# Bucketed attention, a SiLU MLP and routed experts on one core: the first head's projections in two PSUM tiles, the next projection and the V loads later, and one pair's casts on GpSimd

## The chip, the core and the metric

The kernel runs on one core of a Trainium2 chip. The metric is device time in microseconds (us) of one execution, from the first instruction to the last.

## The reference, cut to what matters

Three stages follow each other. The change is in the first, and there in the work on the first of eight pairs of heads.

```python
B, H, S, D = 2, 8, 768, 64                              # attention, proj is (64, 6)
q_bits = (einsum('bhsd,dk->bhsk', q, proj) > 0)         # 6 sign bits per query
k_bits = (einsum('bhsd,dk->bhsk', k, proj) > 0)         # and per key
mask   = q_bucket[:, :, :, None] == k_bucket[:, :, None, :]   # all 6 bits equal
scores = where(mask, q @ k.T / sqrt(D), -1e9)
attn   = exp(scores - max) / (sum + 1e-9)
x      = attn @ v                                       # to (1536, 512)
x      = silu(x @ w_in) @ w_out                         # 512 -> 2048 -> 512
# then tokens with x @ w_skip > 0 go through the best of 8 experts, others pass unchanged
```

## The kernel before, in words

**Stages.** `attention` (L267 to L586) makes the attention output in SBUF, split into a rounded part and a remainder. The MLP and the experts follow, with their weights streamed in. TensorE, VectorE (DVE), ScalarE (ACT), GpSimd (POOL) and SyncE (SP, which issues most of the loads) each take their own instructions in the order of a queue.

**Pairs, units, steps.** Two heads make a pair; eight pairs (`i`), each with two halves of 384 queries, make 16 units. A unit has six steps: three tiles of 128 queries for each of two heads. The very first unit does its three tiles of head 0 first and then those of head 1 (L372); later units alternate the heads. So steps 0 to 2 are head 0 of pair 0 and steps 3 to 5 its head 1. A pair takes 12 steps.

**Scores.** To keep float32 precision, q and k are split: `kh` and `k2` are casts of k, `kl` is what the cast left off; `qa` and `qb` are casts of q, `ql` the remainder (`prep_op`, L306). A score group (`em_S`, L377) has two halves: part 0 multiplies Q1 with K1 (cast and remainder of k, 128 rows), part 1 multiplies Q2 with K2 (remainder of q with the cast of k, 64 rows, and under them 24 mark rows). The mark rows do the masking: the sign bits of query and key stand there as large numbers, such that keys of another bucket get a score far below all others. The result lies in a PSUM tile "S" of which there are two (L383), so group n + 2 needs the tile of group n, which its exponential empties.

**Marks.** For pairs from 1 on, `prep_proj` (L335) multiplies q and k of both heads by the signed projections into one PSUM tile "pj" of the ring "T" (three buffers, shared with the transposes), `marked` (L343) turns it on VectorE into marks in an SBUF tile "mb", and `prep_rows` (L346) copies the mark rows into Q2 and K2 with small DMAs on SyncE's queue. Head 0 of pair 0 has a way of its own (L490 to L504): three matmuls into a tile "pd" (K's two halves in partitions 64 and up, and 96 and up; Q's first half in partitions 0 and up), whose marks VectorE writes straight into Q2 and K2. Head 1 of pair 0, and the second half of the queries, use `prep_proj(0)` and `prep_rows(0)`: K's rows of head 1 in two DMAs, Q's rows of head 1, then Q's second half for both heads.

**Softmax.** `em_soft` (L391): the row maximum `mx` and the bias `bs` on VectorE, the exponential P on ScalarE. `em_T` (L406) transposes P in six matmuls, two steps behind the scores; a half is copied out by ScalarE, the other by VectorE. `em_PV` multiplies with V, six to eight steps behind the scores of a unit.

**Order.** The calls are written out by hand. Ahead of the loop of steps: the loads of pair 0, 29 matmuls on a zero tile (`em_busy`, whose result nobody reads), head 0's projections and casts, its marks, `prep_load(1)`, six more such matmuls, part 0 of group 0, the two ScalarE casts of head 1, `prep_proj(0)`, `prep_rows(0)`, `load_v(0)`, `load_v(1)`, head 1's GpSimd work. In step s the loop calls `em_S(s)` (part 1 alone for step 0), the first half of `em_T(s - 2)`, the casts listed in `PRE`, `em_soft(s)`, then in step 1 `k2` and `kl` of head 1 of pair 0, in steps 0 and 1 four matmuls of `em_busy`, and the second half of `em_T`. `PRE` (L519) lists for pair 1 the steps 2, 4, 6, 8 for `kh` and `qa` of either head, all on ScalarE; `POST` lists the rest. At the end of step 0 the loop calls `prep_load(2)` (L572), whose tiles are those of pair 0 (two buffers, L282). The framework adds the semaphores: a tile is overwritten when the last reader of what was in it is done, also where that reader is called later in the program than the load.

Of the kernel before, what the change touches and what calls it, by code (L numbers as in the profile page):

```python
# [9 lines left out]
F32 = mybir.dt.float32  # L10
# [9 lines left out]
P = 128  # L20
BIG = 2.0 ** 40
NB = 6
# [4 lines left out]
def kernel(  # L27
# [16 lines left out]
    nc = tc.nc  # L44
    B, H, D, S = qT.shape
# [5 lines left out]
    HQ = S // 2  # L51
    QT = HQ // P
    SC = 1.0 / float(D) ** 0.5
    NM2 = 4 * NB
    NK2 = D + NM2
# [11 lines left out]
    def opened(name, bufs=1, space=None, side=None):  # L67

        kw = {"reuse_waits": "tile"} if space in (None, PSUM) else {}
        if space is not None:  # L70
            kw["space"] = space
        if side is not None:
            kw["side"] = side
        st = ExitStack()
        return st.enter_context(tc.tile_pool(name=name, bufs=bufs, **kw)), st
# [25 lines left out]
    prj, c_m = (ct[:, 0:32], ct[:, 32:64]), ct[:, 64:66]  # L101
# [165 lines left out]
    def attention(hook):  # L267
# [4 lines left out]
        psTV, psTV_st = opened("a_psTV", space=PSUM, side="right")  # L272
# [17 lines left out]
        def load_v(i):  # L290
            vts[i] = mainp.tile([P, KT, 2, D], F32, name="v", bufs=3)
            nc.sync.dma_start(vts[i], vt[divmod(i, NP)])
# [6 lines left out]
        def own(hd):  # L299
            return slice(hd * D, (hd + 1) * D)  # L300

        def pieces(n):

            return [slice(c, c + 192) for c in range(0, n, 192)]

        def prep_op(i, hd, what, eng):  # L306

            ks, qs = raws[i]
            if what == "scale":
                nc.scalar.mul(ks, ks, SC)  # L310
                return
            Q1, K1, Q2, K2 = ops[i]
            r, o = own(hd), own(1 - hd)
            if what == "k2" and i:
                nc.sync.dma_start(K2[0:D, hd].bitcast(F32), K1[r, hd].bitcast(F32))
            elif what == "qb" and i:
                nc.sync.dma_start(Q1[o, hd].bitcast(F32), Q1[r, hd].bitcast(F32))
            elif what in ("kh", "k2"):
                dst = K1[r, hd] if what == "kh" else K2[0:D, hd]
                nc.scalar.activation(dst, ks[r], AF.Copy, scale=1.0 if i else SC)  # L320
            elif what in ("qa", "qb"):
                dst = Q1[r if what == "qa" else o, hd]
                (nc.scalar.copy if eng is nc.scalar else eng.tensor_copy)(dst, qs[r])  # L323
            elif what == "kl":
                h = K1[r, hd].bitcast(F32)
                if i:
                    for c in pieces(S):
                        eng.tensor_tensor(K1[o, hd, c], ks[r, c], h[:, c], op=ALU.subtract)  # L328
                else:
                    eng.scalar_tensor_tensor(K1[o, hd], ks[r], SC, h, op0=ALU.mult, op1=ALU.subtract)  # L330
            else:
                for c in pieces(S):
                    eng.tensor_tensor(Q2[0:D, hd, c], qs[r, c], Q1[r, hd, c].bitcast(F32), op=ALU.subtract)  # L333

        def prep_proj(i):  # L335

            ps = psTV.tile([P, HQ], F32, tag="T", name="pj", bufs=3)
            for j in range(4):
                t = raws[i][1 - j // 2]
                nc.tensor.matmul(ps[32 * j:32 * j + 32], prj[j // 2], t[:, (j % 2) * HQ:(j % 2 + 1) * HQ], start=True, stop=True)  # L340
            marked(mks[i], ps, slice(0, P))

        def marked(dst, ps, r):  # L343
            nc.vector.tensor_scalar(dst, ps[r], c_m[r, 0:1], c_m[r, 1:2], op0=ALU.is_gt, op1=ALU.mult)

        def prep_rows(i):  # L346
            mb = mks[i].bitcast(F32)
            Q1, K1, Q2, K2 = ops[i]

            def row_q(half, h0=0):  # L350
                sl = slice(half * HQ, (half + 1) * HQ)
                nc.sync.dma_start(Q2[D:NK2, h0:2, sl].bitcast(F32),
                                  mb[32 * half:32 * half + NM2].unsqueeze(1).to_broadcast([NM2, 2 - h0, HQ]))

            def row_k(hd, half):
                sl = slice(half * HQ, (half + 1) * HQ)
                nc.sync.dma_start(K2[D + 2 * NB * hd:D + 2 * NB * (hd + 1), hd, sl].bitcast(F32),
                                  mb[64 + 32 * half + 2 * NB * hd:64 + 32 * half + 2 * NB * (hd + 1)])

            if i:  # L360
                row_k(0, 0)
                row_q(0)
                row_k(0, 1)
            row_k(1, 0)
            row_k(1, 1)
            if i == 0:
                row_q(0, 1)
            row_q(1)
# [103 lines left out]
        def em_busy(n):  # L472

            for _ in range(n):
                nc.tensor.matmul(bs, busy, busy, start=True, stop=True)
# [12 lines left out]
        em_busy(29)  # L488

        Q1, K1, Q2, K2 = ops[0]  # L490
        ps = psTV.tile([P, HQ], F32, tag="T", name="pd", bufs=3)
        for j in (2, 3, 0):
            t = raws[0][1 - j // 2]
            nc.tensor.matmul(ps[32 * j:32 * j + 32], prj[j // 2][own(0)], t[own(0), (j % 2) * HQ:(j % 2 + 1) * HQ],
                             start=True, stop=True)
        prep_op(0, 0, "kh", nc.scalar)
        prep_op(0, 0, "qa", nc.scalar)
# [1 line left out]
        prep_op(0, 0, "qb", nc.gpsimd)  # L499
        prep_op(0, 0, "ql", nc.gpsimd)  # L500
        prep_op(0, 0, "k2", nc.scalar)
        marked(Q2[D:NK2, 0, 0:HQ], ps, slice(0, NM2))
        for c in range(2):
            marked(K2[D:D + 2 * NB, 0, c * HQ:(c + 1) * HQ], ps, slice(64 + 32 * c, 64 + 32 * c + 2 * NB))  # L504
        prep_load(1)
        em_busy(6)
        em_S(0, (0,))
        prep_op(0, 1, "kh", nc.scalar)
        prep_op(0, 1, "qa", nc.scalar)
        prep_proj(0)  # L510
        prep_rows(0)
        load_v(0)
        load_v(1)
        prep_op(0, 1, "qb", nc.gpsimd)
        prep_op(0, 1, "ql", nc.gpsimd)
        prep_op(1, 0, "scale", nc.scalar)
        nc.gpsimd.memset(K2s[1][D:D + 32].bitcast(F32), 0.0)

        PRE = [[(c[j], j // 2, w, nc.scalar) for j, w in enumerate(("kh", "qa", "kh", "qa"))]  # L519
               for c in ((1, 3, 5, 7), (2, 4, 6, 8))]  # L520

        POST = [[(c[j], j // 4, w, None if w in ("k2", "qb") else nc.gpsimd)
                 for j, w in enumerate(("k2", "kl", "qb", "ql") * 2)]
# [2 lines left out]
        for s in range(NS + PU + 4):  # L526
            i, m = divmod(s, 2 * PU)
            nxt = i + 1 < B * NP
            if nxt and m == 0:
                prep_alloc(i + 1)  # L530
            if s < NS:
                em_S(s, (0, 1) if s else (1,))
            if 0 <= s - 2 < NS:
                em_T(s - 2, 0)
            for mm, *op in PRE[i == 0]:
                if nxt and mm == m:
                    prep_op(i + 1, *op)
            w, pm = divmod(s, PU)
            u, k = (w - 1, pm - 2) if pm >= 2 else (w - 2, pm + 4)
            pv = 0 <= u < len(units)  # L540

            if pv and k % 2:
                em_PV(u, k - 1)
                em_PV(u, k)
            if s < NS:
                em_soft(s)
            if s == 1:
                prep_op(0, 1, "k2", nc.scalar)
                prep_op(0, 1, "kl", nc.vector)
            if s < 2:  # L550
                em_busy(4)
            if 0 <= s - 2 < NS:
                em_T(s - 2, 1)
            if pv:
                if k == 0:
                    em_rc(u)
                if k == (1 if u + 1 < len(units) else 3):
                    rbs[u] = em_r(u)
                if k == KT - 1:
                    xs[u] = em_out(u)  # L560
                if k == 3 and u:
                    em_x(u - 1, xs.pop(u - 1), rbs.pop(u - 1), nc.gpsimd)
            if nxt:
                if m == (1 if i else 5):
                    prep_proj(i + 1)
                for mm, *op in POST[i == 0]:
                    if mm == m:
                        prep_op(i + 1, *op)
                if m == (4 if i else 8):
                    prep_rows(i + 1)  # L570
                if m == 0 and i + 2 < B * NP:
                    prep_load(i + 2)  # L572
                if m == (9 if i else 11) and i + 2 < B * NP:
                    prep_op(i + 2, 0, "scale", nc.scalar)
                if m == 11 and i + 2 < B * NP:
                    load_v(i + 2)
                if m == 11 and i + 2 == B * NP:
                    top_st.close()
            if s == NS - 2 * PU:
                ev_st.close()  # L580
            hook(s - NS)
            if s == NS - 1:
                psS_st.close()
# [278 lines left out]
    with tc.manual_schedule():  # L862
# [128 lines left out]
        ps = ps_tile("pr", [P, 512], "O3")  # L991
# [251 lines left out]
        with tc.If(cnt_max > P):  # L1243
            with tc.For_i(0, NE, 1) as e:
                with tc.For_i(P, NTOK, P) as r0, tc.tile_pool(name="ovf", bufs=1) as op:
# [9 lines left out]
                    for c in range(2):  # L1255
                        ph = psE.tile([P, DM], F32, tag="H", name="oh", bufs=3)
                        for j in range(2):
                            w = op.tile([P, PIECE], F32, name="ow", bufs=3)
# [8 lines left out]
                    for j in range(4):  # L1267
                        w = op.tile([P, PIECE], F32, name="ow", bufs=3)
# [71 lines left out]
```

## Time and profile before

| what | value |
|---|---|
| median of 3 runs | 614.03 us (613.46 to 614.95) |
| profiled execution, its own time | 613.4 us |
| its span (first to last instruction) | 611.6 us |
| TensorE matmul busy | 599.7 us, 98% |
| VectorE, ScalarE, GpSimd busy | 77%, 66%, 29% |

The profile is of one execution. "Busy" counts time in which an instruction of the engine was under way; matmuls are pipelined and their ends are modelled, so a busy TensorE isn't one at its peak. The chain is followed back from the last instruction, each step to what released it. A line such as L388 is a line of the kernel; the line of a helper stands for all its calls. Times of the trace count from the start of the span.

### The profile page before, as it was taken

The page shows a single profiled execution, that of the slowest core. Times are in us where ns is not written, and L with a number is a line of the kernel's source. Part 1 is how long each engine was busy: PE and PEld are TensorE (multiplying, and loading weights), DVE is VectorE, ACT ScalarE, POOL GpSimd, SP SyncE. Part 2 cuts the span into 40 slices and gives each one's busy share as a digit, 9 for nine tenths or more (in the row PEclk, how much of TensorE's full clock was granted, in tenths as well). Part 3 has the DMA queues.
Part 4 walks back from the last instruction along what each step waited for, and adds up shares of the span by engine and source line. Part 5 has one row for each costly group of instructions (what it writes and reads, how often), then busy time and mean ns, then how long its engine had stood idle before and what let it go on. Part 6 is the DMA issues. An engine that isn't in the chain of part 4 may idle for free.

```text
span 611.6 us, 9694 instructions
## 1 busy us (share of the span) xinstructions
PE 599.7 (98%) x3302; PEld 464.7 (76%) x3302; DVE 473.2 (77%) x901; ACT 406.5 (66%) x680; POOL 176.7 (29%) x257
## 2 busy tenths in 40 slices
PE   8899999999999999999999999999999999999996
PEld 5767666766767766888888888888888887788885
DVE  6877787888787776999847985548876559899993
ACT  6978788888878895666544346343445466788882
POOL 5536546472735133100000000300000408247401
PEclk9999999999999999999999999999999999999999
DMA  4533542525213324566333000014321548999930
GB/s 127 154 114 83 185 125 55 165 61 149 67 53 90 108 83 146 179 188 207 129 126 137 1 1 1 1 62 146 103 104 69 126 135 264 349 403 407 405 140 29
DMA packets 30983, 83.74 MB, mean 137 GB/s; under 512 B 6102, under 2 KB 9622, under 8 KB 30802
## 3 DMA queue, kind: packets, MB, share of 16 engines
q1 hardware_dynamic: 28834, 79.07, 39.3%
q0 software_dynamic: 1952, 3.92, 1.9%
q8 instruction: 26, 0.43, 0.3%
q14 instruction: 27, 0.22, 0.1%
q10 hardware_dynamic: 144, 0.11, 0.1%
HBM read 67.92 MB, written 8.50 MB: 125 GB/s over the span
## 4 chain that ended last, share of the span: by engine, by line
PE 89%; ACT 3%; DVE 3%; DMA 2%; issue 2%; POOL 1%; POOLq 0%; ACTq 0%; DVEq 0%
PE ph L611 21%; PE o L654 14%; PE S L388 11%; PE pv L428 11%; PE T L414 10%; PE o L645 7%; PE eh L1112 5%; PE ey L1134 4%; ACT P L402 1%; PE pj L340 1%; PE tr L1089 1%; DMA id_d<-tk,slot 1%; DMA eidr<-id_d 1%; POOL id_d L766 1%; DVE wlo L254 1%
## 5 line engine op out<-in xcount | busy, mean ns | idle before, releaser
L254 DVE TENSOR_TENSOR wlo<-wraw,whi 128x1024 fp32r<-128x1024 f32 x100 | 119.1, 1221 | 6.7 <-ACT whi L251 6.3
L402 ACT ACTIVATE P<-S,bs 128x768 f32<-128x768 f32 x96 | 95.5, 994 | 27.1 <-DVE bs L400 25.4
L617 ACT ACTIVATE g<-ph 128x512 f32<-128x512 f32 x48 | 28.7, 599 | 119.0 <-PE ph L611 115.1
L251 ACT CAST whi<-wraw 128x1024 fp32r<-128x1024 f32 x100 | 101.5, 1052 | 5.2 <-DVE wraw L225 3.1
L398 DVE TENSOR_REDUCE mx<-S 128x1 f32<-128x768 f32 x96 | 91.1, 949 | 11.1 <-PE S L388 8.8
L388 PE MATMUL S<-K,Q 88*128 88x384 f32 (+1 forms) x384 | 92.3, 361 | 3.2 <-ACT P L402 3.1
L414 PEld LDWEIGHTS T<-ident,P 128*128 128x128 f32 x576 | 67.9, 140 | 30.9 <-ACT PT L417 22.1
L414 PE MATMUL T<-ident,P 128*128 128x128 f32 x576 | 88.6, 277 | 0.2 <-ACT PT L417 0.2
L619 DVE TENSOR_TENSOR gl<-g,gh 128x512 fp32r<-128x512 f32 x48 | 33.6, 700 | 55.9 <-ACT gh L618 55.8
L428 PE MATMUL pv<-PT,v 128*64 128x384 f32 x384 | 72.3, 498 | 0.0
L388 PEld LDWEIGHTS S<-K,Q 88*128 88x128 f32 (+1 forms) x384 | 62.7, 191 | 11.8 <-ACT P L402 5.9
L419 DVE COPY PT<-T 128x384 f32<-128x384 f32 x85 | 47.0, 553 | 22.5 <-PE T L414 22.4
L766 POOL DMA_INDIRECT id_d<-tk,slot x12 | 16.3, 1360 | 145.9 <-DVE pre L776 142.5
L417 ACT COPY PT<-T 128x384 f32<-128x384 f32 x107 | 50.5, 479 | 7.2 <-PE T L414 6.9
L611 PE MATMUL ph<-xhi,whi 128*128 128x512 f32 x192 | 52.1, 393 | 0.0
L611 PE MATMUL ph<-xlo,whi 128*128 128x512 f32 x192 | 51.4, 389 | 0.0
L611 PE MATMUL ph<-xhi,wlo 128*128 128x512 f32 x192 | 51.3, 389 | 0.0
L328 POOL TENSOR_TENSOR K<-raw,K 64x192 fp32r<-64x192 f32 x56 | 31.6, 593 | 53.9 <-ACT K L320 28.9
L667 DVE CUSTOM_DVE_ANT_0 junk<-x,gwb 128x512 bf16<-128x512 f32 x72 | 45.3, 688 | 0.0
L333 POOL TENSOR_TENSOR Q<-raw,Q 64x192 fp32r<-64x192 f32 x64 | 36.1, 592 | 28.2 <-ACT Q L323 26.6
L428 PEld LDWEIGHTS pv<-PT,v 128*64 128x64 f32 x384 | 23.4, 136 | 25.7 <-issue 25.6
L611 PEld LDWEIGHTS ph<-xlo,whi 128*128 128x128 f32 x192 | 36.0, 188 | 7.6
(197 smaller groups left out, 1068.4 us busy)
## 6 DMA issues: line engine op xcount, KB each, us to landing
wraw<-in_w_dram SPq DMA_DIRECT2D x64, 512.0 KB
w<-in_mw_dram SPq DMA_DIRECT2D x32, 512.0 KB
v<-in_vt_dram SPq DMA_DIRECT2D x8, 384.0 KB
rb<-r_d SPq DMA_DIRECT2D x32, 96.0 KB
x_d<-x SPq DMA_DIRECT2D x12, 256.0 KB
out_dram<-x SPq DMA_DIRECT2D x12, 256.0 KB
raw<-in_kT_dram SPq DMA_DIRECT2D x7, 384.0 KB
raw<-in_qT_dram SPq DMA_DIRECT2D x7, 384.0 KB
```

Source lines behind the costliest of these rows:

```text
L251: nc.scalar.copy(hi[:, sl], t[:, sl])
L254: eng.tensor_tensor(lo[:, sl], t[:, sl], hi[:, sl].bitcast(F32), op=ALU.subtract)
L388: nc.tensor.matmul(ps[:, c, 0:HQ], q_[0:n, hd, q0:q0 + P], k_[0:n, hd, c * HQ:(c + 1) * HQ], start=first, stop=not first)
L398: nc.vector.tensor_reduce(mx[:, 0:1], ps[:, :, 0:HQ], axis=AX.XY, op=ALU.max, negate=True)
L402: nc.scalar.activation(pt.rearrange("p (a b) -> p a b", a=2), ps[:, :, 0:HQ], AF.Exp, bias=bs_[:, 0:1], scale=bs_[:, 1:2], accum_out=st_su ...
L414: nc.tensor.transpose(ps[:, j], pt[:, k * P:(k + 1) * P], ident)
L417: nc.scalar.copy(dst, ps)
L419: nc.vector.tensor_copy(dst, ps)
L428: nc.tensor.matmul(st_pv[u][hd * D:(hd + 1) * D], vts[i][:, k, hd], st_PT[u][:, hd, k], start=(k == 0), stop=(k == KT - 1))
L611: nc.tensor.matmul(p_[:, 0:c1 - c0], w[:, k * P:(k + 1) * P], x[:, k, t0 * P + c0:t0 * P + c1], start=(q == 0), stop=(q == len(ops3) - 1))
L654: nc.tensor.matmul(acc[t], g[:, (t - t0) * P:(t - t0 + 1) * P], w[:, DM:PIECE], start=(f == 0 and q == 0), stop=(f == NF - 1 and q == 2))
L667: nc.vector.tensor_tensor_reduce(junk, xts[t], pools["gwb_t"][:, c], op0=ALU.mult, op1=ALU.add, scale=1.0, scalar=0.0, accum_out=L[:, t, c ...
```

## The change

It has five parts: the tile "pd" becomes two, `pk` for K's two matmuls and `pq` for Q's; K's marks are called before Q's; `prep_proj(0)`, `prep_rows(0)` and the two V loads move from ahead of the loop into step 1, behind `em_soft(1)`; the busy matmuls become 2 (from 6) ahead of group 0 and 4 in step 1 alone (from 4 in each of steps 0 and 1); and `qa` of pair 1's two heads goes from ScalarE to GpSimd.

```diff
         Q1, K1, Q2, K2 = ops[0]
-        ps = psTV.tile([P, HQ], F32, tag="T", name="pd", bufs=3)
+        pk, pq = [psTV.tile([P, HQ], F32, tag="T", name="pd", bufs=3) for _ in range(2)]
         for j in (2, 3, 0):
             t = raws[0][1 - j // 2]
-            nc.tensor.matmul(ps[32 * j:32 * j + 32], prj[j // 2][own(0)], t[own(0), (j % 2) * HQ:(j % 2 + 1) * HQ],
+            nc.tensor.matmul((pk if j else pq)[32 * j:32 * j + 32], prj[j // 2][own(0)], t[own(0), (j % 2) * HQ:(j % 2 + 1) * HQ],
                              start=True, stop=True)
...
-        marked(Q2[D:NK2, 0, 0:HQ], ps, slice(0, NM2))
         for c in range(2):
-            marked(K2[D:D + 2 * NB, 0, c * HQ:(c + 1) * HQ], ps, slice(64 + 32 * c, 64 + 32 * c + 2 * NB))
+            marked(K2[D:D + 2 * NB, 0, c * HQ:(c + 1) * HQ], pk, slice(64 + 32 * c, 64 + 32 * c + 2 * NB))
+        marked(Q2[D:NK2, 0, 0:HQ], pq, slice(0, NM2))
         prep_load(1)
-        em_busy(6)
+        em_busy(2)
         em_S(0, (0,))
         prep_op(0, 1, "kh", nc.scalar)
         prep_op(0, 1, "qa", nc.scalar)
-        prep_proj(0)
-        prep_rows(0)
-        load_v(0)
-        load_v(1)
         prep_op(0, 1, "qb", nc.gpsimd)
...
-        PRE = [[(c[j], j // 2, w, nc.scalar) for j, w in enumerate(("kh", "qa", "kh", "qa"))]
-               for c in ((1, 3, 5, 7), (2, 4, 6, 8))]
+        PRE = [[(c[j], j // 2, w, (nc.scalar, e)[j % 2]) for j, w in enumerate(("kh", "qa", "kh", "qa"))]
+               for c, e in (((1, 3, 5, 7), nc.scalar), ((2, 4, 6, 8), nc.gpsimd))]
...
             if s == 1:
+                prep_proj(0)
+                prep_rows(0)
+                load_v(0)
+                load_v(1)
                 prep_op(0, 1, "k2", nc.scalar)
                 prep_op(0, 1, "kl", nc.vector)
-            if s < 2:
                 em_busy(4)
```

## Rows read from the trace of the kernel before

**Rows 1.** The page, part 4: shares of the chain that ended last.

```profile
PE 89%; ACT 3%; DVE 3%; DMA 2%; issue 2%; POOL 1%; POOLq 0%; ACTq 0%; DVEq 0%
```

**Rows 2.** That chain, 0 to 110 us: start, us, what.

```profile
9.46 0.68 DVE mb L344
...
13.61 0.84 ACT K L320
...
16.71 0.97 PE S L388 x4
...
24.26 0.96 PE S L388 x4
```

**Rows 3.** TensorE matmuls in order: start, us, what, count, idle before.

```profile
6.39 0.82 PE L475 MATMUL bs<-busy 128*128 128x128 bf16 x6
6.97 0.99 PE L388 MATMUL S<-K,Q 128*128 128x384 f32 x2
7.89 1.51 PE L340 MATMUL pj<-raw,ct 128*32 128x384 f32 x8
9.32 0.66 PE L388 MATMUL S<-K,Q 88*128 88x384 f32 x2
...
10.04 0.94 PE L388 MATMUL S<-K,Q 128*128 128x384 f32 x4
...
12.58 0.98 PE L388 MATMUL S<-K,Q 128*128 128x384 f32 x4 [1.36 <-ACT P L402]
...
13.97 1.17 PE L388 MATMUL S<-K,Q 128*128 128x384 f32 x4
```

**Rows 4.** TensorE weight loads of the score groups' second halves, steps 0 and 3.

```profile
9.32 0.35 PEld L388 LDWEIGHTS S<-K,Q 88*128 88x128 f32 x2 [1.24 <-POOL Q L333]
...
14.52 0.30 PEld L388 LDWEIGHTS S<-K,Q 88*128 88x128 f32 x2 [0.28 <-issue]
```

**Rows 5.** VectorE in order: K's marks, then the maxima of steps 1 and 3.

```profile
7.20 1.40 DVE L344 TENSOR_SCALAR K<-pd,ct 12x384 fp32r<-12x384 f32 x2
...
11.26 0.94 DVE L398 TENSOR_REDUCE mx<-S 128x1 f32<-128x768 f32 x1
...
15.18 0.96 DVE L398 TENSOR_REDUCE mx<-S 128x1 f32<-128x768 f32 x1
16.17 0.20 DVE L400 SCALAR_TENSOR_TENSOR bs<-mx 128x2 f32<-128x2 f32 x1
```

**Rows 6.** ScalarE in order: the exponential of step 3, a cast for pair 1.

```profile
16.92 1.00 ACT L402 ACTIVATE P<-S,bs 128x768 f32<-128x768 f32 x1
...
18.42 0.83 ACT L323 CAST Q<-raw 64x768 fp32r<-64x768 f32 x1
```

**Rows 7.** GpSimd in order: cast and remainder of head 0's q.

```profile
5.06 1.40 POOL L323 CAST Q<-raw 64x768 fp32r<-64x768 f32 x1 [3.73 <-DMA raw<-in_qT_dram]
6.54 2.24 POOL L333 TENSOR_TENSOR Q<-raw,Q 64x192 fp32r<-64x192 f32 x4
```

**Rows 8.** SyncE's queue in order: issues from 3.9 to 16 us.

```profile
3.94 0.43 SPq L286 DMA_DIRECT2D raw<-in_qT_dram  x1
10.17 1.73 SPq L357 DMA_DIRECT2D K<-mb  x2
11.94 1.61 SPq L352 DMA_DIRECT2D Q<-mb  x2
13.60 0.98 SPq L292 DMA_DIRECT2D v<-in_vt_dram  x2
14.76 0.33 SPq L286 DMA_DIRECT2D raw<-in_kT_dram  x1
...
15.71 0.55 SPq L315 DMA_DIRECT2D K<-K  x1
```

**Rows 9.** Two stretches: us, busy (count) of PE, PEld, DVE, ACT, POOL, clock, DMA share, GB/s.

```profile
5.00:10.00 5.00, 5.00 (x27) 1.93 (x24) 3.34 (x5) 3.93 (x5) 4.79 (x7) 1.00 0.56 177
13.40:13.60 0.20, 0.20 (x3) 0.20 (x2) 0.01 (x1) 0.18 (x2) 0.00 (x0) 1.00 0.39 92
```

## The prediction

> **What bounds the kernel now.** I read the page's chain first: 89% of it is TensorE, 3% each VectorE and ScalarE [rows 1]. Then the same chain in order of time. The change touches only the first 27 us, and there the chain isn't TensorE's. It goes through the first pair's mark on VectorE (9.46 to 10.14 us) and the first row maximum behind it, then through ScalarE: the two exponentials of groups 0 and 1, the cast k2 of head 1 (13.61 to 14.45), and so to score group 4 on TensorE (16.71) [rows 2]. From 24.26 on it is TensorE's [rows 2], as the 89% has it for the whole. So what this start loses or wins goes to the end nearly one for one. Last I read each engine's order of time from 3 to 17 us, and SyncE's queue.
>
> I write S(n), mx(n), P(n), T(n) for scores, maximum, exponential and transposes of step n. Steps 0 to 2 are head 0, steps 3 to 5 head 1. The two halves of S(0) stand apart, at 6.97 and 9.32 [rows 3].
>
> **The change part by part.**
>
> *Two tiles and K's marks first.* The three marks cost about 0.7 us each; the one for Q, which waited for the last projection matmul, goes last, so all end about 0.7 us sooner than 8.60 [rows 5]. This gains nothing by itself: the second half of S(0) also needs Q's remainder from GpSimd, which ends at 6.54 + 2.24 = 8.78 [rows 7]. A third buffer of the T ring is taken; it is free again long before T(0). Value 0.
>
> *The next projection off the way of S(0).* The weight load of S(0)'s second half sat idle 1.24 us, put down to that remainder, but the remainder was done at 8.78 and the load began at 9.32 [rows 4]: between them the eight pj matmuls (7.89 + 1.51 = 9.40) held TensorE [rows 3]. Without them it starts at about 8.84: 0.48 us sooner. mx(0), which stood behind the mark till 10.14 [rows 2], moves to between 9.55 and 9.80.
>
> The two ends differ by TensorE's clock. The granted column reads 1.00 in this stretch too [rows 9], so I take the level from durations: two S matmuls took 0.99 at 6.97, four took 0.94 at 10.04 [rows 3]. The engine was at 1.2 GHz till about 9.5 us, although it was busy all of 5 to 10 us [rows 9], and at 2.4 GHz after. The change empties it before that moment: fourteen busy matmuls become six (six took 0.82 us [rows 3]) and pj is gone, so from about 7.6 to 8.84 it stands. I take it that the clock rises later than before, some time before S(2). Then S(0)'s half takes 0.9 in place of 0.66, S(1) about 1.5 in place of 0.94, pj 1.5 as before. P(0) and P(1) come 0.15 to 0.2 us sooner; with the early rise 0.5. Value 0.2.
>
> *The projection, its mark and the rows after the second softmax.* This is the costly part. S(3) is the first group of head 1, and its second half reads mark rows that prep_rows copies: two for K, then one for Q. Before, the mark ended at 10.14, and the row issues began at 10.17 and (Q's) 11.94; Q's packets were through by 13.6 [rows 8, 9], so S(3) did not wait for them but for k2, and its second half began at 14.52 [rows 4]. Now the mark stands on VectorE behind mx(1) (before 11.26 to 12.20 [rows 5]): with the early clock all of that is 0.5 sooner, and a bias of 0.2 and the mark's 0.68 end at 12.6; with the late one pj ends only at 12.4 (S(1) to 11.1, then its 1.5, overlapping by 0.2), the mark at 13.1 to 13.2. From a mark's end to Q's row in place are 0.03 + 1.77 + about 1.7 = 3.5 us [rows 8, 9]. Alone this puts S(3)'s second half at 16.1 to 16.7, in place of 14.52.
>
> But the rows and V loads are also moved past two other loads of SyncE's queue. prep_load(2) is called at the end of step 0; it overwrites pair 0's raw tiles and so waits for their last readers, k2 of head 1 among them (end 14.45, load issued at 14.76 [rows 2, 8]). Before, the rows and V were called ahead of it, now they are called in step 1, behind it. Does the queue keep the order of the calls? The V loads speak for it: nothing holds them back (fresh buffers), SyncE issued nothing from 4.37 to 10.17, yet they were issued at 13.60, behind the rows [rows 8]. So I take it that the rows now stand behind a load that waits for k2. k2 ends 0.2 us sooner, at 14.25; the load is issued 0.31 later, the next instruction 0.95 after that (14.76 to 15.71), so the first row at 15.5, and Q's row is in place 1.77 + 1.7 later, at 19.0 [rows 8, 9]. S(3)'s second half is then 4.5 us late.
>
> *What is late next.* TensorE takes its work in order, so T(1) and S(4) stand behind S(3). From the start of S(3)'s second half to P(3) are 0.62 (it ended at 15.14), 0.04, mx 0.96, bias 0.2 and handovers: 1.9 us [rows 3, 5]. P(3) was at 16.92, 2.4 after 14.52, since ScalarE was held by P(2) [rows 6]; so 0.5 of the 4.5 is swallowed. Now 19.0 + 1.9 = 20.9, 4.0 later. S(5) needs the S buffer that P(3) empties, S(6) follows on TensorE behind S(5), T(3) and pair 1's projection, and from there the offsets are the old ones. Loss 4.0; with the early clock, 3.65. I take 3.9.
>
> The Trainium skill's "DMA: Bandwidth & Descriptors", in its anatomy of one DMA, puts a fixed cost of about 2.0 us on a transfer. The rows here give 1.7 from the start of the issue to the last packet, and the measured number is used; by the page's, an estimate, Q's row would be 0.3 us later, and the sum 4.2.
>
> *Casts to GpSimd.* Two casts of 0.83 us leave ScalarE, one in step 4 (18.42 [rows 6]) and one in step 8; GpSimd took 1.40 for such a cast [rows 7]. At 16.71 (S(4)) and from 24.26 (S(8)) the chain is TensorE's [rows 2]; so a gain between 0 and, if ScalarE were the bound, 1.7. I take 0, nearest to the chain's rows. What GpSimd casts is read by scores from step 12 on only, so 1.4 us there delays nothing.
>
> **Sum.** 613.4 (profiled execution; its span is 611.6) + 3.9 = 617.3. The median of the three timed runs is 614.03, 0.6 higher, so for a median: 617.9.
>
> **The rivals.**
>
> *The rows go ahead of prep_load(2).* The queue could set aside a load whose buffer isn't free; nothing in the trace shows such a case, nor rules it out. Then S(3)'s second half is at 16.1 to 16.7, P(3) at 18.0 to 18.6 in place of 16.92, loss 1.1 to 1.7: 615.1 to 615.7. Chance 0.25.
>
> *The clock falls back in the wait.* In the forecast TensorE stands from about 14.1 to 19.0. Before, its longest pause here was 1.4 us (before S(2)), and the clock stayed up. Should it fall, T(1), S(4), T(2) and S(5) run at half the rate: S groups 1.5 in place of 0.94, so some 2 us more in all: 619.5 to 620. Chance 0.10. The skill's "TensorE: Matmul & The Clock Gate", part 1, has it that idleness returns the clock to the lower level; no row here shows a fall.
>
> *Not slower.* S(3) is served in time. The one mechanism is the rows' arrival: it would need them in place by about 14.0, so the first issued by 10.5. Then the 0.5 of S(0) and up to 0.8 of a cast on ScalarE are kept: 612.7 to 613.5. Against it, the mark can't end before mx(1) and the bias do, at 11.9. Chance 0.10, mostly for what I have overlooked.
>
> **How the numbers follow.** Forecast 0.55, its own range 617.0 to 618.7 (the clock early or late, and half a microsecond either way in what P(3)'s slack of 0.5 swallows). About 0.2%, 1.2 us, is what a measurement of this kernel can tell from no change, so slower begins at 615.3. Slower: the forecast (less 0.02 if some of it is absorbed), the clock's fall 0.10, half of the rows-first case 0.13: 0.76. Same: the other half 0.12, 0.02, and 0.03 of the last rival: 0.17. Faster 0.07. The range reaches down to the rows-first case less 0.3, 614.8, and up to the edge of the clock's fall, 619.6.
>
> **What would show it.** Right: SyncE issues pair 2's raw loads ahead of the first marks' rows, the rows between 15 and 18.5 us; S(3)'s second half begins at 18.5 to 19.2, and P(3) near 20.9; S(0)'s second half at 8.84; the steps from S(6) on keep their old distances. Wrong: rows issued at 12.6 to 13.2 (first rival), S matmuls at the 1.2 GHz durations after 19 us (second), S(3) begun by 14.5 (third). If P(3) is 4 us late and the end is not, the start isn't passed on one for one.

## The result, and the profile after

The changed kernel takes 619.6 us (median of 6 runs, 618.26 to 620.37); the kernel before, run beside it, 613.76 (6 runs, 611.92 to 614.95). The ratio is 1.0104, interval 1.0091 to 1.0118: slower by 5.6 to 7.2 us, where 3.9 was forecast. The profiled execution of after took 619.53, that of before 613.4: 6.1 apart.

The forecast let the old distances hold from S(6) on; S(8) is the last row of the chain that was read. It starts at 30.30 in place of 24.26 [rows 2], 6.04 later. After it nothing is won or lost: the first small transpose of the sums (L439), at 28.7 us of before, is 6.06 late, and the last matmul 6.07. All 6.1 us arise ahead of S(8), in the stretch that was read.

SyncE's queue after, in order of time (start, duration, what was issued), against [rows 8]:

```profile
14.19 0.33 SPq L286 DMA_DIRECT2D raw<-in_kT_dram  x1
14.68 0.33 SPq L286 DMA_DIRECT2D raw<-in_qT_dram  x1
15.05 1.73 SPq L357 DMA_DIRECT2D K<-mb  x2
16.82 1.61 SPq L352 DMA_DIRECT2D Q<-mb  x2
18.48 0.98 SPq L292 DMA_DIRECT2D v<-in_vt_dram  x2
19.58 0.54 SPq L315 DMA_DIRECT2D K<-K  x1
```

The rows stand behind pair 2's raw loads, as forecast. What sets the time of those loads, and the mark that the rows copy, on ScalarE and VectorE:

```profile
13.32 0.84 ACT L320 ACTIVATE K<-raw 64x768 fp32r<-64x768 f32 x1
```

```profile
6.03 1.38 DVE L344 TENSOR_SCALAR K<-pd,ct 12x384 fp32r<-12x384 f32 x2
7.44 0.67 DVE L344 TENSOR_SCALAR Q<-pd,ct 24x384 fp32r<-24x384 f32 x1
...
12.04 0.67 DVE L344 TENSOR_SCALAR mb<-pj,ct 128x384 fp32r<-128x384 f32 x1
...
20.00 0.96 DVE L398 TENSOR_REDUCE mx<-S 128x1 f32<-128x768 f32 x1 [4.40 <-PE S L388]
20.99 0.43 DVE L400 SCALAR_TENSOR_TENSOR bs<-mx 128x2 f32<-128x2 f32 x1
```

The first load follows the end of k2 (14.16) by 0.03. The mark was ready at 12.71, so the rows waited 2.3 us in the queue for nothing but their place in it. TensorE's matmuls after, against [rows 3]; the last column is idle time before, and what ended it:

```profile
6.73 0.62 PE L388 MATMUL S<-K,Q 128*128 128x384 f32 x2 [0.58 <-POOL Q L323]
8.25 2.26 PE L388 MATMUL S<-K,Q 88*128 88x384 f32 x6 [0.90 <-ACT Q L323]
10.44 1.51 PE L340 MATMUL pj<-raw,ct 128*32 128x384 f32 x8
...
12.25 1.63 PE L388 MATMUL S<-K,Q 128*128 128x384 f32 x4
...
14.76 0.60 PE L388 MATMUL S<-K,Q 128*128 128x384 f32 x2
18.98 0.98 PE L388 MATMUL S<-K,Q 88*128 88x384 f32 x2 [3.63 <-DMA Q<-mb]
19.76 1.48 PE L414 MATMUL T<-ident,P 128*128 128x128 f32 x6
20.89 1.63 PE L388 MATMUL S<-K,Q 128*128 128x384 f32 x4
...
23.45 1.62 PE L388 MATMUL S<-K,Q 128*128 128x384 f32 x4
...
30.30 0.97 PE L388 MATMUL S<-K,Q 128*128 128x384 f32 x4 [0.85 <-ACT P L402]
```

S(3)'s second half waits 3.63 us for Q's mark rows. Behind the wait S(4) and S(5) take 1.63 and 1.62 us: the same four matmuls take 0.97 at 30.30. The granted clock says why. Stretches of 2 us; behind the stretch and its length stand busy time (count) of PE, PEld, DVE, ACT and POOL, then the clock, DMA share and GB/s, as in [rows 9]:

```profile
8.00:10.00 2.00, 1.75 (x6) 1.78 (x6) 0.84 (x2) 1.09 (x2) 1.94 (x4) 0.50 0.01 3
...
12.00:14.00 2.00, 2.00 (x10) 1.90 (x10) 1.75 (x4) 1.76 (x3) 1.47 (x2) 0.50 0.00 0
...
16.00:18.00 2.00, 0.00 (x0) 0.00 (x0) 0.00 (x0) 0.88 (x2) 2.00 (x4) 1.00 0.83 317
18.00:20.00 2.00, 1.01 (x4) 0.95 (x5) 0.00 (x1) 0.00 (x0) 1.86 (x4) 0.53 0.44 91
20.00:22.00 2.00, 2.00 (x9) 2.00 (x8) 1.85 (x3) 0.96 (x2) 1.40 (x3) 0.50 0.98 359
```

The column reads 0.50, the lower of the two levels (1.2 GHz), in two stretches: from about 7.9 to 14.7, beginning in the pause of 0.90 us ahead of 8.25, and from about 18.1 to 24.9, beginning in the long wait. From 25 us on it is up. Two more views of after: P(3) on ScalarE, and what GpSimd took for its remainder and for one of the casts it was given:

```profile
21.52 0.99 ACT L402 ACTIVATE P<-S,bs 128x768 f32<-128x768 f32 x1 [0.40 <-DVE bs L400]
```

```profile
6.76 2.24 POOL L333 TENSOR_TENSOR Q<-raw,Q 64x192 fp32r<-64x192 f32 x4
...
31.53 0.82 POOL L323 CAST Q<-raw 64x768 fp32r<-64x768 f32 x1
```

### The profile page after: what moved, and what is told of

It is laid out like the page before. It is cut to its first block, busy times and chain, and to the rows that moved or that the text cites. A ratio compares the mean times of both kernels' runs of the same rounds, so it can differ in the third digit from the quotient of the medians.

```text
span 617.7 us, 9679 instructions
## 1 busy us (share of the span) xinstructions
PE 603.3 (98%) x3294; PEld 468.4 (76%) x3294; DVE 473.9 (77%) x901; ACT 405.7 (66%) x678; POOL 174.4 (28%) x259
## 5 line engine op out<-in xcount | busy, mean ns | idle before, releaser
L402 ACT ACTIVATE P<-S,bs 128x768 f32<-128x768 f32 x96 | 95.5, 994 | 28.5 <-DVE bs L400 25.5
L616 ACT ACTIVATE g<-ph 128x512 f32<-128x512 f32 x48 | 28.7, 599 | 119.0 <-PE ph L610 115.2
L388 PE MATMUL S<-K,Q 88*128 88x384 f32 (+1 forms) x384 | 94.9, 370 | 6.1 <-DMA Q<-mb 3.6
L414 PEld LDWEIGHTS T<-ident,P 128*128 128x128 f32 x576 | 69.8, 143 | 31.1 <-ACT PT L417 22.7
L414 PE MATMUL T<-ident,P 128*128 128x128 f32 x576 | 90.5, 281 | 0.2 <-ACT PT L417 0.2
L388 PEld LDWEIGHTS S<-K,Q 88*128 88x128 f32 (+1 forms) x384 | 65.1, 197 | 13.5 <-POOL K L328 3.9
L428 PEld LDWEIGHTS pv<-PT,v 128*64 128x64 f32 x384 | 23.4, 136 | 25.7 <-issue 25.5
```

The costliest lines, as they stand in the source:

```text
L388: nc.tensor.matmul(ps[:, c, 0:HQ], q_[0:n, hd, q0:q0 + P], k_[0:n, hd, c * HQ:(c + 1) * HQ], start=first, stop=not first)
L402: nc.scalar.activation(pt.rearrange("p (a b) -> p a b", a=2), ps[:, :, 0:HQ], AF.Exp, bias=bs_[:, 0:1], scale=bs_[:, 1:2], accum_out=st_su ...
L414: nc.tensor.transpose(ps[:, j], pt[:, k * P:(k + 1) * P], ident)
L428: nc.tensor.matmul(st_pv[u][hd * D:(hd + 1) * D], vts[i][:, k, hd], st_PT[u][:, hd, k], start=(k == 0), stop=(k == KT - 1))
```

## The experiments

In each, "before" is the kernel before, run beside it on the same chip. Theory: the queue's order makes S(3) late, and a clock that falls in the wait adds the rest. Rivals: another part of the change costs, or the pause isn't what lowers the clock.

**The move alone.** Before, with `prep_proj(0)`, `prep_rows(0)` and the V loads moved as in the change, and no other part of it.

```diff
-        prep_proj(0)
-        prep_rows(0)
-        load_v(0)
-        load_v(1)
...
             if s == 1:
+                prep_proj(0)
+                prep_rows(0)
+                load_v(0)
+                load_v(1)
```

> The kernel before with only that move: prep_proj(0), prep_rows(0) and the two V loads called in step 1 behind the softmax. Six busy matmuls ahead of group 0 and four in each of steps 0 and 1 as before, old marks, casts on ScalarE. Theory: the whole loss is here, rows issued behind pair 2's raw loads, S(3)'s second half at 18.5 to 19.2, and the clock falls in the wait of about 4 us as in the changed kernel: time 618.8 to 620.0. Rival 2 (the fewer busy matmuls are what costs): within 1.5 us of the kernel before.

618.6 us (6 runs), ratio 1.0083 (1.0062 to 1.0105), a little under what I had. S(3)'s second half begins at 19.24, put down to Q's rows, S(8) at 29.36, 5.1 late. The clock fell behind the wait (S(4) took 1.63), but was up again sooner than in after (S(5) took 1.27, there 1.62). The move brings most or all of the loss.

**All but the move.** After, with those four calls back ahead of the loop.

> The changed kernel with prep_proj(0), prep_rows(0) and the two V loads called ahead of the loop again; the two tiles, the order of the marks, the fewer busy matmuls and the casts on GpSimd stay. Theory: the move carries the whole loss; S(3)'s second half begins at 14.4 to 14.8, S(8) at 24.0 to 24.6, time 613.3 to 614.3, the same as before within what can be measured. Rival 2 (fewer busy matmuls, so a lower clock up to 14.6 us): 615 to 617. A gain of the casts would show as 612.5 to 613.2.

614.08 us (12 runs), ratio 1.0011 (0.9997 to 1.0024). Two tiles, K's marks first, fewer busy matmuls and GpSimd's casts together cost nothing that these runs can tell.

**The queue's order alone.** Before, with pair 2's raw loads called ahead of the rows; projection and mark stay where they were.

```diff
         prep_proj(0)
+        prep_load(2)
         prep_rows(0)
...
-                if m == 0 and i + 2 < B * NP:
+                if m == 0 and i and i + 2 < B * NP:
```

> The kernel before with one edit: prep_load(2) is called ahead of prep_rows(0), in place of the end of step 0. The projection, its mark and everything else stay where they were. Theory (the queue order is the cost, the mark's place is not): the rows are issued behind pair 2's raw loads, which wait for k2 of head 1 (14.45 us), so from about 15.7; S(3)'s second half begins at 19.0 to 19.5 in place of 14.52, and TensorE stands some 4 us before it; time 617.4 to 619.6, the upper part if the clock falls in the wait. Rival (mark's new place is the cost): 613.5, as before.

619.4 us (6 runs), ratio 1.009 (1.0069 to 1.011). Its SyncE issues, then its matmuls, the last of them S(8):

```profile
14.68 0.33 SPq L286 DMA_DIRECT2D raw<-in_kT_dram  x1
...
17.31 1.61 SPq L352 DMA_DIRECT2D Q<-mb  x2
```

```profile
19.53 0.98 PE L388 MATMUL S<-K,Q 88*128 88x384 f32 x2 [4.76 <-DMA Q<-mb]
...
21.44 1.63 PE L388 MATMUL S<-K,Q 128*128 128x384 f32 x4
...
30.07 0.98 PE L388 MATMUL S<-K,Q 128*128 128x384 f32 x4 [0.85 <-ACT P L402]
```

One call put elsewhere, no instruction added or taken away, gives the loss of the whole change (S(8) 5.81 late, in after 6.04). Where the queue holds the rows back, the later projection and mark aren't needed for the loss; what they cost without it is seen next.

**The order mended in the changed kernel.** After, with `prep_load(2)` called in step 1 behind the V loads.

> The changed kernel, with pair 2's raw loads called in step 1 behind the rows and V loads, in place of the end of step 0. Theory (the queue order holds the rows, and the wait lets the clock fall): the rows are issued right behind the mark, at about 12.75 us, Q's row is in place at 16.2 to 16.4, the second half of S(3) begins there instead of at 18.98, P(3) at about 18.3; S(8) begins at 25.5 to 26.0 (before 24.26, changed kernel 30.30), and the time is 1.2 to 1.8 us over the kernel before: 615.0 to 615.6. Rival 1 (the mark's new place on VectorE is the cost, the queue is not): S(3) stays at 18.5 to 19, time about 619.6. Rival 2 (the low clock alone, rows absorbed): S(3) earlier but the time stays within 1 us of the changed kernel's.

616.36 us (9 runs), ratio 1.0048 (1.0032 to 1.0063). The first row on SyncE, and S(3)'s second half:

```profile
12.64 1.73 SPq L357 DMA_DIRECT2D K<-mb  x2
```

```profile
16.64 0.59 PE L388 MATMUL S<-K,Q 88*128 88x384 f32 x2 [1.61 <-DMA Q<-mb]
```

This is the forecast's first rival made true, and S(3) came out where that put it (16.1 to 16.7). The time did not: I had 615.0 to 615.6, with S(8) at 25.5 to 26.0. It is at 26.36, 2.1 late as S(3) is: P(3)'s slack swallowed nothing, since VectorE's bias ahead of it took 0.68 in place of 0.20 [rows 5]. S(1), the projection and S(2) ran at the lower level here as in after, so the 2.1 are not the mark's new place alone. About half of the loss is back. In this profile 1.1 us more arise between 520 and 540 us; I have no cause for them.

**The move to step 0.** After, with the four calls in step 0 behind `em_soft(0)` (so ahead of `prep_load(2)`), and the busy matmuls of before.

> The changed kernel with prep_proj(0), prep_rows(0) and the V loads called in step 0 behind em_soft(0), so one step sooner and ahead of prep_load(2); busy matmuls as before (6, 4, 4). Theory: the mark ends at 11.5 to 12.0, Q's row is in place at 15.0 to 15.5, S(3)'s second half begins 0.5 to 1.0 later than before and the slack of 0.5 swallows most: 613.4 to 614.4. Rival (any mark behind a maximum costs its full delay): 614.4 to 615.2.

615.08 us (12 runs), ratio 1.0027 (1.0014 to 1.004). The rows are issued at 11.18; S(3)'s second half begins at 15.66, no longer put down to the rows:

```profile
15.66 0.59 PE L388 MATMUL S<-K,Q 88*128 88x384 f32 x2 [0.29 <-ACT K L320]
```

I had 613.4 to 614.4, too low. The time lies in the rival's range, but not by its mechanism: S(3) waits for k2, not for the rows. The projection now stands on TensorE between S(0) and S(1), which starts at 10.70; the second softmax and k2 follow, k2 at 14.72 in place of 13.61 [rows 2], and S(8) is at 25.37. Both are 1.1 late. But before, the projection stood ahead of S(1) too, and here S(1) took 1.63, in before 0.94 [rows 3]: the clock rose later in this execution, and how much of the 1.1 is the projection's new place isn't shown. S(9), at 27.24, is another 0.5 late, as with the casts alone below.

**Busy matmuls in the wait.** After, with 32 of them between the halves of S(3).

```diff
-                em_S(s, (0, 1) if s else (1,))
+                if s == 3:
+                    em_S(s, (0,))
+                    em_busy(32)
+                em_S(s, (0, 1) if s not in (0, 3) else (1,))
```

> The changed kernel, with 32 matmuls on the zero tile between the two halves of S(3), so that TensorE works in the wait for the rows. Theory: S(3)'s second half still begins at about 18.95, but the granted clock does not go to 0.50 at 18.4; S(4), S(5) take 0.95 in place of 1.63, S(8) begins at 28.2 to 28.6 in place of 30.30, time 617.4 to 617.9 (1.7 to 2.2 us under the changed kernel). Rival 2 (clock alone makes the loss): time back to within 1 us of the kernel before. Rival 3 (the clock falls whatever the engine does, or does not matter because VectorE and ScalarE set the pace): no change from 619.6.

619.05 us (6 runs), ratio 1.0093 (1.0074 to 1.0113), over the 617.4 to 617.9 that I had. The fillers ended at 16.92, and 2.24 us of the wait stayed empty. In the profiled execution (617.89) the clock stayed up: S(3) at 19.16, S(4) 0.95, S(8) at 28.78, 1.5 us ahead of after's although S(3) was 0.2 behind. The six runs fall into three of 617.9 to 618.6 with a mean granted clock (1 is full speed throughout) of 0.994 or 0.995, and three of 619.5 to 620.1 with 0.989 or 0.990. The profile is of the first kind; that the clock fell with the wait in the second is likely, and not shown.

**Busy from the start.** The same with 40, the busy matmuls of before, and 12 between the halves of S(0).

> The changed kernel with TensorE kept at work on the zero tile up to S(3)'s second half: 6 busy matmuls ahead of group 0, 12 between the halves of S(0), 4 in each of steps 0 and 1, and 40 between the halves of S(3). Theory (loss = late rows about 4, plus the low clock about 2): S(3)'s second half at 18.9 to 19.3 as in the changed kernel, no stretch at 0.50 behind 10 us, S(8) at 28.2 to 28.8, median 617.2 to 618.0, and the runs lie closer together than with 32 in the wait alone (617.9 to 620.1). Rival (the spread is not the clock's): 618.5 to 619.5 as with 32.

618.26 us (6 runs), ratio 1.0077 (1.0056 to 1.0099). A miss: 2.33 us of the wait stayed empty here too, and in the profiled execution (618.71) the clock fell after it; 20 to 22 us read 0.59, S(8) was at 29.55.

```profile
19.43 0.59 PE L388 MATMUL S<-K,Q 88*128 88x384 f32 x2 [2.33 <-DMA Q<-mb]
20.49 1.63 PE L388 MATMUL S<-K,Q 128*128 128x384 f32 x4
```

Here too the runs part by the mean clock: 617.5 and 617.6 with 0.999, and four of 617.8 to 619.5, the profiled one among them, with 0.994 or 0.995.

**The wait filled.** The same with 68 in place of the 40.

> The changed kernel with the busy matmuls of before (6 and 4 and 4), 12 between the halves of S(0), and 68 in the wait inside S(3), where the run with 40 still left 2.3 us of it empty. Theory (queue order about 4.4 us, the rest the clock that falls in the wait): the 28 more fill about 1.5 us more, so under 1 us of idle time is left before S(3)'s second half at 19.2 to 19.5; S(4) and S(5) then take 0.95 to 1.0 us in place of 1.63, S(8) starts at 28.5 to 28.9, and the time is 617.2 to 617.9, some 2 us under the changed kernel. Rival (the pause is not what lowers the clock): S(4) at 1.63 again, S(8) at 29.5 to 30.3, 618.5 to 619.6.

617.99 us (5 runs, 617.33 to 619.28), ratio 1.0093 (1.0073 to 1.0113). Its matmuls:

```profile
14.60 3.97 PE L475 MATMUL bs<-busy 128*128 128x128 bf16 x68
19.62 0.59 PE L388 MATMUL S<-K,Q 88*128 88x384 f32 x2 [1.04 <-POOL Q L333]
...
20.62 0.95 PE L388 MATMUL S<-K,Q 128*128 128x384 f32 x4
...
28.83 0.97 PE L388 MATMUL S<-K,Q 128*128 128x384 f32 x4 [0.85 <-ACT P L402]
```

This trace has the queue's cost with the clock up: S(3)'s second half 5.1 us late (0.6 more than in after, 0.33 of it since k2 ended later), S(8) 4.57 late. The 0.5 in between is what P(3)'s slack swallows. The timed medians don't part this kernel from after: the intervals overlap, and two of the five runs (618.84, 619.28) lie in after's range. Their mean clock is 0.995, that of the other three (617.3 to 618.0) 0.997 or 0.998, so in these two the clock may have fallen after all; no profile shows it.

**All but the move, with the busy matmuls of before.**

> The changed kernel with the move undone (as in the run with that alone, 614.08) and the busy matmuls as before: 6 ahead of group 0, 4 in each of steps 0 and 1. What is left of the change: two tiles, order of marks, casts on GpSimd. Theory (these three lie beside other work): 613.0 to 613.9, same as before. Rival (the casts shorten ScalarE's part of the chain up to 24 us): 612.2 to 612.9. If it is 0.4 us or more under 614.08, the fewer busy matmuls had a price of their own.

613.66 us (12 runs), ratio 1.0009 (0.9995 to 1.0023). Nothing, as without them. But its profiled execution (614.8) shows the clock fall with no long wait at all, in 1.56 us ahead of S(2):

```profile
12.70 1.65 PE L388 MATMUL S<-K,Q 128*128 128x384 f32 x4 [1.56 <-ACT P L402]
```

```profile
14.00:16.00 2.00, 2.00 (x10) 1.90 (x9) 1.45 (x3) 1.53 (x3) 0.00 (x0) 0.50 0.79 241
```

```profile
25.59 0.97 PE L388 MATMUL S<-K,Q 128*128 128x384 f32 x4 [0.80 <-ACT P L402]
```

S(2) is 0.12 late, S(8) 1.33: a fall of the clock costs about 1.2 us here, with the rows in time.

**The casts alone.** Before, with pair 1's `qa` on GpSimd and nothing else.

> The kernel before, with pair 1's two casts per group on GpSimd and nothing else of the change. Theory (the chain is TensorE's where they lie, worth 0): S(8) at 24.0 to 24.5, 613.0 to 614.2, within 0.1% of before. Rival (ScalarE bounds steps 4 to 8, so two casts of 0.83 us come free): S(8) 0.8 to 1.7 us sooner, at 22.5 to 23.4, 611.8 to 612.6. Rival (GpSimd's 1.4 us casts are late for the scores that read them, or hold up its own later work): 0.5 us or more over before.

613.95 us (11 runs), ratio 1.0018 (1.0002 to 1.0034): if anything slower. **A longer filler ahead of S(2)** went with it: before, with 16 busy matmuls in step 1 in place of 4.

> The kernel before with 16 busy matmuls in step 1 in place of 4, so that TensorE's 1.36 us pause before S(2) is mostly filled. Theory (the clock falls in pauses of this size in some executions): executions at 614 and over become rarer, and the median falls to 612.2 to 613.2 where before is at 613.0 to 613.8; the fastest executions stay where they are, about 612. Rival (before's spread comes from elsewhere): the same median as before within 0.3 us. If the added matmuls delay S(2), 12.58 becomes later and the time rises by as much.

612.34 us (11 runs), ratio 0.9997 (0.9986 to 1.0008): the same. Its longest run was 613.5, and 4 of before's 21 were over 613.9, so long times may be rarer; no version here beats before. The profiles of these two agree within 0.1 us up to S(8) and can be laid side by side. S(8) and S(9), the casts first, the filler second:

```profile
22.76 0.97 PE L388 MATMUL S<-K,Q 128*128 128x384 f32 x4 [0.72 <-ACT P L402]
...
24.62 0.96 PE L388 MATMUL S<-K,Q 128*128 128x384 f32 x4 [0.24 <-ACT P L402]
```

```profile
22.78 0.97 PE L388 MATMUL S<-K,Q 128*128 128x384 f32 x4 [0.85 <-ACT P L402]
...
24.17 0.96 PE L388 MATMUL S<-K,Q 128*128 128x384 f32 x4
```

S(9) comes 0.45 later with the casts moved, and that stays to the end. Ahead of it VectorE's bias of step 7 took longer, in the casts' kernel first:

```profile
22.80 0.59 DVE L400 SCALAR_TENSOR_TENSOR bs<-mx 128x2 f32<-128x2 f32 x1
```

```profile
22.70 0.16 DVE L400 SCALAR_TENSOR_TENSOR bs<-mx 128x2 f32<-128x2 f32 x1
```

GpSimd worked beside it in both, so what made it longer is open. The same stands in the profiles of all but the move and of the move to step 0 (bias 0.59 both times; S(9) 1.86 and 1.87 behind S(8)). In after S(9) follows S(8) by 1.38 us, as in before: there the casts cost nothing.

## Why the prediction was wrong

**The failed step: the clock.** The sum took the clock as up from some time before S(2) on and carried no term for its falling in the wait; that stood as a rival with 0.10, "some 2 us more in all: 619.5 to 620". It fell, and the time came out there. TensorE then worked without a pause from S(3)'s second half (18.98) to S(6) (26.45), 7.47 us, most of them at the lower level; with the wait filled and the clock up the same stretch took 5.36 (19.62 to 24.98). So the path to S(6) was TensorE's own slow work, and not P(3), by which the sum went. The parts add up: S(3)'s second half is 4.43 late (18.95 on the weight loads, where [rows 4] have 14.52), less the 0.5 that P(3)'s slack would swallow is 3.9, the forecast's figure; S(8) is 6.04 late, so the clock's term is 2.1, the difference of 7.47 and 5.36 too. The filled wait shows the two apart, 4.57 at S(8) with the clock up and 5.1 at S(3), and the times with 32 fillers fall into two groups. By the same sum the fall cost 1.3 in the queue's order alone and 0.9 in the move alone, where the lower level ended sooner: its price varies with the execution. My ground was that the longest pause of before, 1.4 us, left the clock up. That says nothing of 3.6 us, and I should have given this case more than half the chance. The Trainium skill's "TensorE: Matmul & The Clock Gate", part 1, which I cited, says that idleness brings the lower level back; the trace agrees (0.50 from within the 3.63 us on).

**The queue: right.** The rows wait behind `prep_load(2)`, which waits for k2; that order alone gives the loss. S(3)'s second half was forecast at 19.0 and is at 18.95, but by two errors that cancel, which is luck. The first row came at 15.05, not 15.5: the load followed k2 by 0.03, where I took the 0.31 of before, in which SyncE was still issuing the V loads (till 14.58 [rows 8]) when k2 ended. And from the issue of Q's row to its use were 2.16 us (16.82 to 18.98), not the 1.7 that I read from the last packet [rows 9]. The last packet was through 1.7 us behind the issue here too (at 18.5); the reader began 0.45 later, so a packet's end isn't yet the moment at which the reader is released. The 2.0 of the Trainium skill's "DMA: Bandwidth & Descriptors", in its anatomy of one DMA, which I set aside for the row, was nearer, though the Trainium skill gives it there for GpSimd's path, and these rows are SyncE's.

**The clock ahead of S(2): wrong, without effect.** I had it rise late. It was up by 6.73 (two S matmuls in 0.62) and fell at 7.9, and S(0)'s second half and S(1) ran slow as in the forecast, for another reason; that k2 ended at 14.16, where 14.25 was forecast, is luck in part.

**S(0)'s second half: wrong by 0.6, without effect.** I put it at 8.84, behind the whole remainder of q. It began at 8.22, when the remainder's last part still ran (to 9.00) and Q's mark, now last, had just ended (8.11). So it needs the mark and only the first parts of the remainder.

**P(3) and the old distances.** P(3) is at 21.52, not 20.9: half of S(3), mx, bias and handovers took 2.54 in place of 1.9, 0.36 more of it the half at the lower clock and 0.23 the bias on VectorE (0.43 in place of 0.20 [rows 5]), and so the slack was used up. From S(8) on the old distances hold (6.04 to 6.07 late throughout), from S(6) on as forecast (26.45, also 6.04).

**Marks and tiles 0: right** within 0.2% (614.08 beside 613.5). **Casts 0: right in after.** One took GpSimd 0.82 us, not the 1.40 of [rows 7]. Alone they cost some 0.45 us by the profile, and so they do in the profiles of two other runs, a side that I had not bounded.

**Left open:** in what share of executions the clock falls. In after's own six runs the mean clock doesn't order the times (0.994 at 620.05 and 620.37, 0.987 at 619.53), so the times vary for other reasons as well; the first rise, told at the end, may be one.

## What to carry to other kernels

When a call is moved, list what it now stands behind on the queue that issues its DMAs: a load into a reused buffer waits for the last reader of the old data, and everything called after it waits too. When a forecast makes TensorE stand for longer than any pause in the trace, price both clock levels behind the pause and give the lower one most of the chance: here it came behind all three empty waits over 3.6 us. Take a DMA's delay from the issue to the start of its reader, not to its last packet.

## What the runs showed of the hardware

The length of a pause alone doesn't tell whether the clock falls. It stayed up behind 1.90 us ahead of S(2) (all but the move; S(2) then took 0.97) and behind 2.24 us (32 fillers), and it fell with 0.90 (after), 1.56 (all but the move, with the busy matmuls of before) and 2.33 (40 fillers). It fell in, or right behind, each of the three empty waits that were longer: 3.63 (after), 4.20 (the move alone) and 4.76 (the queue's order alone). Once down it stayed so in after till 14.7 and till 24.9 us, although TensorE was busy nearly all of the time from 8.25 and from 18.98 on.

Times differ by the clock's first rise. Before and the kernel with the longer filler are the same up to S(1). In the profile of before S(1) began at 10.04 [rows 3], in the filler's at 8.65, since there more of the matmuls ahead of it ran fast (pj took 0.85 in place of 1.51); S(8) is then 1.48 us sooner, and the profiled times 1.4 apart (612.0, 613.4). The clock column reads 1.00 in both from the start: it does not show this first low stretch, only durations do.
